# Counts copied to SBUF, places one and two pairs later, one transpose per query tile

## The chip, the core and the metric

The kernel runs on one core of a Trainium2 chip. The metric is the device time of one execution in microseconds (us). TensorE multiplies matrices (PE in the rows; PEld is its weight load), VectorE is DVE, ScalarE is ACT, GpSimd is POOL and SyncE (SP) issues most transfers.

## The reference

Causal attention for 8 batches, 12 heads, 448 positions and a head width of 64; its result, 3584 rows of 768, goes through a mixture of 8 experts. Each row picks the expert with the largest logit; its weight is that expert's softmax probability. An expert keeps the 80 rows with the largest weights among those that picked it; the other rows are zero in the output.

```
scores = where(causal, q @ k^T / 8, -1e9);  x = softmax(scores) @ v   # 12 heads side by side: [3584, 768]
expert = argmax(x @ w_gate);  gate_w = softmax(x @ w_gate)[row, expert]
for e in range(8):
    rows = the (at most) 80 rows of expert e with the largest gate_w
    out[rows] = gate_w[rows] * (relu(x[rows] @ w1[e]) @ w2[e])        # 768 -> 1024 -> 768
```

## The kernel before, in words

The work has two parts: attention for 48 head pairs (6 pairs for each of 8 batches), and then the experts, each with at most 80 rows. While attention runs, a table of the best 80 rows of every expert is kept: after each batch its rows are compared with each other and with the table, ranked, and the table is made anew.

**Order of the work.** The order is written out by hand. Every pair has eight slots (main loop, lines 1187 to 1253). Within a slot the loop puts, in this order, transposes of probabilities (`tp`, four groups in slots 0, 1, 1, 4), the product of values (`xp`, slot 5, of the pair two before), VectorE's masking with the row's smallest (`ns`, slots 0 to 4), copies of transposed probabilities (`PT`, ScalarE in slot 1 and VectorE in slot 5), ScalarE's exponentials (`prob`), ScalarE's copy of the finished values (`xu`, slot 6), and then whatever a plan has for that slot; the score products of the next pair end slot 7. Each engine carries out its instructions in that order and waits for what it needs.

**The plan of a batch.** Its steps are placed by the table `STEPS` (line 30; the seventh batch has its own table `EARLY`, the eighth a text list `TAIL`). A number is the slot counted from the end of the batch's last pair, so 42 is the third slot of the sixth pair after it; steps of two batches stand beside each other. The steps that matter:

- `columns`, `parts` (lines 831 and 843): GpSimd writes, for each of four query tiles, three copies of the one-hots of the experts (`oh3`) and five groups of 8 columns with the row's number and its weight in three bf16 parts (`mv`). They are two buffers.
- `r0t`, `r1t`, `r0c`, `r1c` (`expert_rows`, line 856): TensorE turns the one-hots and the weight columns, four transposes each into a bank of PSUM; VectorE copies 24 rows of each to `ex`.
- `rl`, `lt`, `cp`, `ro` (`table_chunk`, line 886): the table's rows against the batch's rows; `cp` counts, for each table row, the batch's rows that go ahead of it. `ro` hands `cp`, in PSUM, on.
- `places`, `places2` (`place`, line 919): VectorE makes one-hots `rm` of the table rows' new places, 80x320 in each half. They exist from the second batch on. They are used by `tn` in slot 74.
- `c3w` to `c0l` (`compare`): the batch's rows with each other (`rn`, `less`). `gt`, `own`, `rank`, `rr`: later rows counted, ranks, and the one-hot of ranks; `gt` and what `own` and `rank` make of it lie in one bank.

**Banks of PSUM.** The pool `ps_g` has four banks with one tag (line 211): `tp`, `rt` (transposed rows of the result, `row_group`, line 715), `xp`, `gp`, `selt`, `rn`, `rl`, `cp`, `gt`, `tn` take them in turn. A new tile waits until all that read the tile four before it are done.

```
STEPS = {... 'r0t': 41, 'r0c': 42, 'r1t': 42, 'r1c': 43, 'rl': 44, 'lt': 46, ... 'cp': 53, 'ro': 53, 'places': 54, ... 'places2': 54, ...}
```

Of the kernel before, what the change touches and what calls it, by code (L numbers as in the profile page):

```python
# [17 lines left out]
P = 128  # L18
# [8 lines left out]
NORMS = [0, 2, 4]  # L27
ROWS0 = [(2, 2), (3, 4), (9, 9), (19, 20)]
ROWS1 = [(27, 28), (35, 36), (36, 38), (40, 41)]
STEPS = {'gp': 20, 'gs': 22, 'lp': 24, 'lg': 25, 'logit': 26, 'shifted': 27, 'chosen': 32, 'sums': 33, 'one_hot': 33, 'columns': 33, 'weight': 35, 'weighted': 36, 'parts': 37, 'r0t': 41, 'r0c': 42, 'r1t': 42, 'r1c': 43, 'rl': 44, 'lt': 46, 'c3w': 49, 'c3l': 50, 'cp': 53, 'ro': 53, 'places': 54, 'c2w': 56, 'c2l': 57, 'places2': 54, 'c1w': 58, 'c1l': 59, 'c0w': 60, 'c0l': 61, 'earlier': 61, 'gt': 65, 'own': 67, 'rank': 67, 'rr': 68, 'tn': 73, 'tab': 74, 'rp': 76, 'row': 78}  # L30
EARLY = {'gp': 18, 'gs': 20, 'lp': 24, 'lg': 25, 'logit': 26, 'shifted': 26, 'chosen': 28, 'sums': 29, 'one_hot': 29, 'columns': 29, 'weight': 30, 'weighted': 30, 'parts': 30, 'r0t': 33, 'r0c': 34, 'r1t': 35, 'r1c': 36, 'rl': 36, 'lt': 38, 'c3w': 40, 'c3l': 41, 'c2w': 41, 'c2l': 42, 'c1w': 42, 'c1l': 43, 'cp': 43, 'ro': 43, 'c0w': 44, 'c0l': 45, 'earlier': 45, 'places': 46, 'places2': 46, 'gt': 46, 'own': 47, 'rank': 47, 'rr': 47, 'tn': 49, 'tab': 49, 'rp': 52, 'row': 53}
THIRD = [0, 0, 2, 2, 4, 6, 8]
THIRD_EARLY = [0, 2, 4, 6, 6, 8, 9]
# [139 lines left out]
def attention_then_moe(  # L173
# [12 lines left out]
    nc = tc.nc  # L186
    B, _, NP, S = qT.shape
    N, D = out.shape
    E = wg.shape[2]
# [3 lines left out]
    NT = (S + P - 1) // P  # L193
# [50 lines left out]
    SL = max(2, min(P, CAP))  # L244
    NSL = (CAP + SL - 1) // SL
    NV = 5

    COUNT = F16 if CAP + S <= 2048 else F32
    ZR = 4
# [4 lines left out]
    OFF, at = {}, 0  # L254
# [49 lines left out]
    for e, which in LAYERS:  # L304
# [4 lines left out]
        k = (K1, K2)[which - 1]  # L309
# [42 lines left out]
        return [lambda j=j, x=x: load_chunk(*got[0], j, x, 2) for j in range(k) for x in range(2)]  # L352


    mv = one_hots = mv_flat = oh_flat = expert_cols = tables = table_rows = None
    identb = before = dec = number = number_after = pnum = tbase = wgd = slots_e = slots_t = None

    tiny = const.tile([P, 1], F32, name="tiny")
# [1 line left out]
    lg = keep.tile([P, NT, (H + 1) * E], F32, name="lg")  # L360
# [35 lines left out]
    def late_constants():  # L396


        def padded(shape, name):
            t = spool.tile(shape, BF16, name=name, tag=name, bufs=1)  # L400
            nc.gpsimd.memset(t, 0.0)
            return t
# [20 lines left out]
                                          wg_sb[j * DH:(j + 1) * DH, i:NP:2, :])  # L423

        def slots():
            nonlocal mv_flat, mv
            mv_flat = padded([P, (NT - 1) * NV * E + 2 * E + P], "mv")
            mv = mv_flat[:, 0:NT * NV * E].rearrange("k (t v e) -> k t v e", v=NV, e=E)

        def operands():  # L430
            nonlocal oh_flat, one_hots, expert_cols, tables, table_rows
            oh_flat = padded([P, (NT - 1) * 3 * E + P], "oh3")
            one_hots = oh_flat[:, 0:NT * 3 * E].rearrange("k (t v e) -> k t v e", v=3, e=E)
            expert_cols = padded([P, 2, NT * P], "ex")
            tables = [[padded([SL, 2 * E + P], f"tab{s}_{i}") for i in range(2)] for s in range(NSL)]
            table_rows = [[padded([P, SL], f"row{s}_{i}") for i in range(2)] for s in range(NSL)]
# [384 lines left out]
    table = []  # L821
    rows_of = {}

    def select_groups(bt):

        b = bt.b
        last = b == B - 1
        sm = lambda name, shape, dt=F32: spool.tile(shape, dt, name=name, tag=name, bufs=1)
# [24 lines left out]

            nc.gpsimd.tensor_copy(sm("held", [P, 1]), bt.rest[:, 0, 0:1])

        def expert_rows(i):
            got = []

            def turn():
                selt = bank([P, NT * P], BF16, "selt")  # L860
                got.append(selt)
                for t in range(NT):
                    src = mv_flat[:, (t * NV + 2) * E:][:, 0:P] if i else oh_flat[:, t * 3 * E:][:, 0:P]
                    nc.tensor.transpose(selt[:, t * P:(t + 1) * P], src, identb)

            def copy():
                (nc.scalar.copy if last else nc.vector.tensor_copy)(bt.ex[0:3 * E, i], got[0][0:3 * E])
            return [turn, copy]


        def compare(t):
            w = (t + 1) * P
# [13 lines left out]
        def table_chunk(s):  # L886
            sn = min(SL, CAP - s * SL)
            got = {}
# [20 lines left out]

            def ranks():  # L910
                if NSL == 1:
                    bt.moves.append((table[s][0], got["cp"], sn))
                    return
                ro = sm(f"ro{s}", [SL, E])
                nc.vector.tensor_scalar(ro[0:sn], got["cp"][0:sn], pnum[0:sn], float(s * SL), op0=ALU.add, op1=ALU.add)
                bt.moves.append((table[s][0], ro, sn))
# [69 lines left out]
        def move(s):  # L986
# [49 lines left out]
            def row():  # L1036
# [3 lines left out]
                if s == NSL - 1:  # L1040
# [1 line left out]
            return [moved_table, one_hot, moved_last, taken] if last else [one_hot, moved, taken, turn, row]  # L1042

        bt.lower, bt.moves = [], []
        r0, r1 = expert_rows(0), expert_rows(1)
        cmp = [compare(t) for t in reversed(range(NT))]
        tabs = [table_chunk(s) for s in range(NSL)] if b else []
        moves = [f for s in range(NSL) for f in move(s)]
        steps = {"columns": columns, "parts": parts, "r0t": r0[0], "r0c": r0[1], "r1t": r1[0], "r1c": r1[1],
                 "places": places, "places2": more_places, "earlier": earlier, "own": own, "rank": rank}  # L1050
        steps.update({"hold": hold, "base": base, **{f"gt{t}": lambda t=t: later_part(t) for t in range(NT)}} if last else {"gt": later})
        for t in range(NT):
# [37 lines left out]
    for b in range(B):  # L1090
        bt = Batch()
# [94 lines left out]
    parts = []  # L1186
    for i, pr in enumerate(pairs):
        bt = pr.bt
# [76 lines left out]
    bt = batches[-1]  # L1265
# [314 lines left out]
```

## Time and profile before

| | us |
|---|---|
| median of 3 runs | 450.36 (448.03 to 450.75) |
| the profiled execution | 449.43 |
| its span, first to last instruction | 447.7 |
| TensorE busy | 428.3 (96%) |
| ScalarE busy | 391.7 (87%) |
| VectorE busy | 383.2 (86%) |
| GpSimd busy | 237.7 (53%) |

Busy times are of the one profiled execution; the rest of its 449.43 us lies around the span. A matmul's end is modelled, so the distance between starts says more of TensorE than the length of a record. Idle time is shown in brackets with what ended it.

### The profile page before, as it was taken

What the parts mean: (1) busy time and instruction counts of PE and PEld (TensorE: products, weight loads), DVE (VectorE), ACT (ScalarE), POOL (GpSimd) and SP (SyncE); (2) the same over time, 40 slices, a digit from 0 to 9 for tenths busy, and PEclk for the clock granted to TensorE, in tenths of its full rate; (3) what the DMA queues carried; (4) which work ended last, traced back from release to release, by engine and by line L of the source; (5) the groups of instructions that cost most, each with busy time, mean ns of one, the idle gap of its engine ahead of it and who ended that gap; (6) DMA issues with size and microseconds to landing.
All of it is one profiled execution on the core that took longest, in us unless ns stands there. A gap on an engine that the chain in (4) does not pass through costs nothing. (4 is left out here: it accounts for less than half of the span.)

```text
span 447.7 us, 15806 instructions
## 1 busy us (share of the span) xinstructions
PE 428.3 (96%) x5830; PEld 332.6 (74%) x5830; DVE 383.2 (86%) x1315; ACT 391.7 (87%) x1069; POOL 237.7 (53%) x360
## 2 busy tenths in 40 slices
PE   7899999999999999999999999999899999999993
PEld 3566777777677777767767776766559999899993
DVE  6777788979879897987999789798879999989992
ACT  5899999989889988988999898888877999899971
POOL 7967818547664843866585284622452126525521
PEclk9899999999999999999999999999989999999997
DMA  6475648758675762866666375379889999999701
GB/s 227 147 272 195 228 157 284 236 169 289 195 239 180 241 228 92 264 210 207 226 224 216 113 266 192 103 253 403 326 294 340 405 409 400 398 414 413 297 26 45
DMA packets 47823, 109.95 MB, mean 246 GB/s; under 512 B 5971, under 2 KB 24403, under 8 KB 47105
## 3 DMA queue, kind: packets, MB, share of 16 engines
q1 hardware_dynamic: 46544, 105.20, 67.0%
q0 software_dynamic: 1056, 3.51, 2.4%
q8 instruction: 46, 0.75, 0.7%
q14 instruction: 33, 0.26, 0.2%
q10 hardware_dynamic: 144, 0.23, 0.2%
HBM read 85.35 MB, written 23.99 MB: 244 GB/s over the span
## 5 line engine op out<-in xcount | busy, mean ns | idle before, releaser
L562 ACT ACTIVATE prob<-ns,nb 128x192 f32<-128x192 f32 (+3 forms) x336 | 175.4, 531 | 17.3 <-DVE nb L558 15.8
L558 DVE CUSTOM_DVE_ANT_0 ns<-sp,mask 128x192 f32<-128x192 f32 (+3 forms) x336 | 134.3, 442 | 23.2 <-PE sp L539 20.8
L596 PE MATMUL tp<-ident,prob 128*128 128x128 f32 x768 | 106.0, 279 | 0.1
L487 POOL TENSOR_TENSOR qk<-qk,qk 128x448 f16<-128x448 f32 x94 | 96.7, 1044 | 5.8 <-DVE qk L515 2.6
L1157 DVE SCALAR_TENSOR_TENSOR wl<-wraw,wh 128x768 f16<-128x768 f32 (+1 forms) x99 | 98.3, 1062 | 1.7 <-POOL wl L1506 1.6
L619 PE MATMUL xp<-PT,vt 128*64 128x448 f32 (+3 forms) x768 | 93.6, 386 | 0.2
L1151 ACT ACTIVATE wh<-wraw 128x768 f16<-128x768 f32 (+1 forms) x99 | 86.6, 936 | 7.4 <-PE hp L1445 5.2
L596 PEld LDWEIGHTS tp<-ident,prob 128*128 128x128 f32 x768 | 85.8, 143 | 2.4 <-ACT PT L601 0.5
L619 PEld LDWEIGHTS xp<-PT,vt 128*64 128x64 f32 x768 | 50.9, 136 | 44.6 <-issue 24.5
L601 ACT COPY PT<-tp 128x512 f32<-128x512 f32 x144 | 76.5, 589 | 7.6 <-PE tp L596 7.1
L539 PE MATMUL sp<-qk 64*128 64x448 f16 (+2 forms) x864 | 68.4, 298 | 2.9 <-POOL qk L487 2.1
L1446 PEld LDWEIGHTS <-wl 128*128 128x128 f16 x678 | 67.7, 100 | 2.3 <-issue 2.2
L1444 PEld LDWEIGHTS <-wh 128*128 128x128 f16 x678 | 68.2, 101 | 0.2 <-issue 0.2
L1445 PEld LDWEIGHTS <-wh 128*128 128x128 f16 x678 | 67.6, 100 | 0.7 <-issue 0.5
L562 ACT ACTIVATION_READ_ACCUMULATOR prob<-ns,nb 128x1 f32 x336 | 66.0, 196 | 0.0
L1490 POOL DMA_INDIRECT out<-yo,idx x8 | 32.7, 4086 | 51.2 <-ACT yo L1487 39.9
L539 PEld LDWEIGHTS <-qk 64*128 64x128 f16 x864 | 36.5, 94 | 17.7 <-issue 2.8
L601 DVE COPY PT<-tp 64x256 f32<-64x256 f32 x144 | 43.5, 327 | 3.2 <-PE tp L596 1.0
L1446 PE MATMUL hp<-xh,wl 128*128 128x80 f16 x336 | 37.8, 202 | 1.2 <-issue 1.2
L1445 PE MATMUL hp<-xl,wh 128*128 128x80 f16 x336 | 37.7, 202 | 0.5 <-issue 0.3
L1444 PE MATMUL hp<-xh,wh 128*128 128x80 f16 x336 | 37.9, 202 | 0.0
L1444 PE MATMUL op<-hh,wh 128*128 128x80 f16 x318 | 36.3, 202 | 0.3 <-issue 0.2
(187 smaller groups left out, 659.3 us busy)
## 6 DMA issues: line engine op xcount, KB each, us to landing
wraw<-w SPq DMA_DIRECT2D x49, 384.0 KB, 9.0
wraw<-w SPq DMA_DIRECT2D x29, 512.0 KB, 9.0
out<-mask SPq DMA_DIRECT2D x56, 192.0 KB, 2.2
qk<-k_t SPq DMA_DIRECT2D x23, 448.0 KB, 3.5
qk<-q_t SPq DMA_DIRECT2D x23, 448.0 KB, 5.0
vt<-v_t SPq DMA_DIRECT2D x24, 384.0 KB, 5.8
xs<-xr SPq DMA_DIRECT2D x42, 192.0 KB, 2.8
wraw<-w SPq DMA_DIRECT2D x24, 256.0 KB, 3.8
```

Of the source, the lines that this page charges most:

```text
L487: sub = lambda e, o, a, b: e.tensor_tensor(out=o, in0=a, in1=b, op=ALU.subtract)
L539: nc.tensor.matmul(pr.sp[t, j], a[rows, p, queries(t)], c[rows, p, FROM[t]:FROM[t] + WIDTH[t]], start=(x == 0), stop=(x == 2))
L558: nc.vector.tensor_tensor_reduce(out=ns, in0=pr.sp[x], in1=m, scale=-1.0 / 8.0, scalar=HUGE, op0=ALU.add, op1=ALU.min, accum_out=nb)
L562: nc.scalar.activation(pr.P[:, OFF[x]:OFF[x] + w], got[0], AF.Exp, bias=got[1], scale=-1.0, accum_out=pr.sums[:, h:h + 1])
L596: nc.tensor.transpose(tp[:, i * P:(i + 1) * P], f, ident)
L601: way(part_of(pr.PT, rows, to, *todims), part_of(got[0], rows, at, *dims))
L619: nc.tensor.matmul(xp[rows, c * P:S], st["vt"][:, c, p * P + j * DH:p * P + (j + 1) * DH], pr.PT[:, j, n0:n0 + w], start=(c == 0), stop=(c ...
L1151: nc.scalar.activation(hi_of[y][:, 0:src.shape[1]], src, AF.Copy, scale=SW)
L1157: nc.vector.scalar_tensor_tensor(out=lo_of[y][:, 0:n], in0=src, scalar=SW, in1=hi_of[y][:, 0:n], op0=ALU.mult, op1=ALU.subtract)
L1444: nc.tensor.matmul(o, wh[:, ws], h[:, c, :], start=begin, stop=False, skip_group_check=True)
L1445: nc.tensor.matmul(o, wh[:, ws], l[:, c, :], start=False, stop=False, skip_group_check=True)
L1446: nc.tensor.matmul(o, wl[:, ws], h[:, c, :], start=False, stop=end, skip_group_check=True)
```

## The change

The table `STEPS` gets other slots for nine steps; `r1t` is gone from it. One-hots and columns share one buffer, 96 columns to a query tile: number columns and weight parts from column 16 on (weight parts at 32), one-hots at 64. For the first six batches one 128-wide transpose per tile turns both; the copies take rows 64 and up, and 32 and up, of the one bank. For the last two batches there are still two sets of four transposes, the one for the one-hots 32 columns wide. In all batches but the last, `ro` is a ScalarE copy of the counts (80x8) to SBUF, and the places read that. In `STEPS` alone the places are moved: their first half from slot 54 to 62, their second half from 54 to 66.

```diff
-STEPS = {... 'r0t': 41, 'r0c': 42, 'r1t': 42, 'r1c': 43, 'rl': 44, 'lt': 46, ... 'cp': 53, 'ro': 53, 'places': 54, ... 'places2': 54, ...}
+STEPS = {... 'r0t': 42, 'r0c': 43, 'r1c': 43, 'rl': 45, 'lt': 47, ... 'cp': 53, 'ro': 54, 'places': 62, ... 'places2': 66, ...}
...
+    CM, CO, CW = 32, 64, 96
...
         def slots():
-            nonlocal mv_flat, mv
-            mv_flat = padded([P, (NT - 1) * NV * E + 2 * E + P], "mv")
-            mv = mv_flat[:, 0:NT * NV * E].rearrange("k (t v e) -> k t v e", v=NV, e=E)
+            nonlocal columns_of, one_hots, mv
+            columns_of = padded([P, (NT - 1) * CW + CO + P], "columns")
+            blocks = columns_of[:, 0:NT * CW].rearrange("k (t c) -> k t c", c=CW)
+            mv = blocks[:, :, CM - 2 * E:CM - 2 * E + NV * E].rearrange("k t (v e) -> k t v e", e=E)
+            one_hots = blocks[:, :, CO:CO + 3 * E].rearrange("k t (v e) -> k t v e", e=E)
...
-        def expert_rows(i):
+        def expert_rows(*which):
             got = []
+            at = [CO, CM]
+            alone = len(which) == 1
 
             def turn():
                 selt = bank([P, NT * P], BF16, "selt")
                 got.append(selt)
+                w = 32 if which == (0,) else P
                 for t in range(NT):
-                    src = mv_flat[:, (t * NV + 2) * E:][:, 0:P] if i else oh_flat[:, t * 3 * E:][:, 0:P]
-                    nc.tensor.transpose(selt[:, t * P:(t + 1) * P], src, identb)
+                    c = t * CW + (at[which[0]] if alone else 0)
+                    nc.tensor.transpose(selt[0:w, t * P:(t + 1) * P], columns_of[:, c:c + w], identb)
 
-            def copy():
-                (nc.scalar.copy if last else nc.vector.tensor_copy)(bt.ex[0:3 * E, i], got[0][0:3 * E])
-            return [turn, copy]
+            def copy(i):
+                r = 0 if alone else at[i]
+                (nc.scalar.copy if last else nc.vector.tensor_copy)(bt.ex[0:3 * E, i], got[0][r:r + 3 * E])
+            return [turn] + [lambda i=i: copy(i) for i in which]
...
             def ranks():
                 if NSL == 1:
-                    bt.moves.append((table[s][0], got["cp"], sn))
+                    ro = got["cp"]
+                    if not last:
+                        ro = sm("ro", [SL, E])
+                        nc.scalar.copy(ro[0:sn], got["cp"][0:sn])
+                    bt.moves.append((table[s][0], ro, sn))
                     return
...
-        r0, r1 = expert_rows(0), expert_rows(1)
+        rows = expert_rows(0) + expert_rows(1) if b >= B - 2 else expert_rows(0, 1)
```

## Rows read from the trace of the kernel before

**Rows 1.** Windows: length, busy us (instructions) of PE, PEld, DVE, ACT, POOL; clock, DMA share, GB/s.

```profile
180.00:220.00 40.00, 39.66 (x448) 28.80 (x448) 35.02 (x155) 36.27 (x116) 24.55 (x43) 1.00 0.66 215
350.00:400.00 50.00, 48.83 (x1047) 48.10 (x1044) 48.19 (x57) 46.31 (x72) 18.78 (x6) 1.00 1.03 403
```

**Rows 2.** Timeline of one pair with places: start, length, engine, line, operation, [idle before, ended by].

```profile
119.03 0.99 DVE L927 SCALAR_TENSOR_TENSOR rm<-cp,pnum,slots_e 80x320 bf16<-80x320 f32 x2
119.28 0.26 PE L546 MATMUL sp<-qk,corner 128*128 128x64 f16 x3
119.94 0.34 DVE L558 CUSTOM_DVE_ANT_0 ns<-sp,mask 128x192 f32<-128x192 f32 x1
120.02 1.04 PE L596 MATMUL tp<-ident,prob 128*128 128x128 f32 x8
120.32 0.46 ACT L562 ACTIVATE prob<-ns,nb 128x192 f32<-128x192 f32 x1 [1.08 <-DVE nb L558]
120.78 1.54 ACT L601 COPY PT<-tp 128x512 f32<-128x512 f32 x3
121.39 0.31 PEld L730 LDWEIGHTS rt<-ident,xu 128*128 128x128 f32 x3 [0.58 <-ACT PT L601]
...
121.98 0.56 DVE L749 TENSOR_TENSOR xr<-rt,sums 128x384 f32<-128x384 f32 x1 [0.47 <-PE rt L730]
...
122.59 0.20 PEld L619 LDWEIGHTS xp<-PT,vt 128*64 128x64 f32 x4 [0.23 <-DVE xr L749]
122.59 1.95 PE L619 MATMUL xp<-PT,vt 128*64 128x448 f32 x16
...
125.73 0.34 DVE L558 CUSTOM_DVE_ANT_0 ns<-sp,mask 128x192 f32<-128x192 f32 x1
...
125.81 0.26 PE L546 MATMUL sp<-qk,corner 128*128 128x64 f16 x3
```

**Rows 3.** Timeline of an earlier pair, TensorE around the turned one-hots and columns.

```profile
107.63 1.04 PE L596 MATMUL tp<-ident,prob 128*128 128x128 f32 x8
...
108.50 0.39 PE L864 MATMUL selt<-identb,oh 128*128 128x128 bf16 x4
...
108.95 0.62 PE L596 MATMUL tp<-ident,prob 128*128 128x128 f32 x4
```

**Rows 4.** Waits: who waited for whom, us in total, times, longest.

```profile
PE rt L730 <- ACT PT L601: 2.3, 7, 0.3
```

**Rows 5.** Instructions on the counts and on the table: ns shortest/median/longest, first and last start.

```profile
L927 DVE SCALAR_TENSOR_TENSOR rm<-cp,pnum,slots_e x14: 530/532/546, 119.0 to 323.5; 80x320 bf16<-80x320 f32 x14
...
L1030 ACT CAST tab<-tn x1: 188/188/188, 317.5 to 317.5; 80x40 bf16<-80x40 f32 x1
```

**Rows 6.** The same view of line 1157, an instruction with two SBUF inputs.

```profile
L1157 DVE SCALAR_TENSOR_TENSOR wl<-wraw,wh x99: 944/951/1226, 312.5 to 436.9; 128x768 f16<-128x768 f32 x57, 128x1024 f16<-128x1024 f32 x42
```

**Rows 7.** Timeline of the pair after that of rows 2.

```profile
126.08 1.80 POOL L515 CAST qk<-qk 128x896 f16<-128x896 f32 x2
...
127.10 0.61 DVE L558 CUSTOM_DVE_ANT_0 ns<-sp,mask 128x448 f32<-128x448 f32 x1
...
129.06 0.48 DVE L992 TENSOR_TENSOR rr<-gt,slots_t 128x320 bf16<-128x320 f32 x1
...
129.84 1.95 PE L619 MATMUL xp<-PT,vt 128*64 128x448 f32 x16
...
132.69 0.36 DVE L558 CUSTOM_DVE_ANT_0 ns<-sp,mask 128x192 f32<-128x192 f32 x1 [1.74 <-PE sp L539]
```

**Rows 8.** GpSimd beside VectorE: timeline at the start, and line 487 over the span.

```profile
4.70 1.16 DVE L487 TENSOR_TENSOR qk<-qk,qk 128x448 f16<-128x448 f32 x2
5.48 0.87 POOL L492 COPY corner<-qk 64x128 f16<-64x128 f16 x2 [1.32 <-DVE qk L487]
...
9.03 0.63 POOL L492 COPY corner<-qk 64x128 f16<-64x128 f16 x2
...
16.33 0.62 DVE L515 CAST qk<-qk 128x896 f16<-128x896 f32 x1
16.48 1.37 POOL L487 TENSOR_TENSOR qk<-qk,qk 128x448 f16<-128x448 f32 x1
...
L487 POOL TENSOR_TENSOR qk<-qk,qk x94: 1032/1040/1366, 7.1 to 286.0; 128x448 f16<-128x448 f32 x94
```

More of the change, by code (lines that the diff above doesn't have):

```diff
@@ L29 @@
 ROWS1 = [(27, 28), (35, 36), (36, 38), (40, 41)]
-STEPS = {'gp': 20, 'gs': 22, 'lp': 24, 'lg': 25, 'logit': 26, 'shifted': 27, 'chosen': 32, 'sums': 33, 'one_hot': 33, 'columns': 33, 'weight': 35, 'weighted': 36, 'parts': 37, 'r0t': 41, 'r0c': 42, 'r1t': 42, 'r1c': 43, 'rl': 44, 'lt': 46, 'c3w': 49, 'c3l': 50, 'cp': 53, 'ro': 53, 'places': 54, 'c2w': 56, 'c2l': 57, 'places2': 54, 'c1w': 58, 'c1l': 59, 'c0w': 60, 'c0l': 61, 'earlier': 61, 'gt': 65, 'own': 67, 'rank': 67, 'rr': 68, 'tn': 73, 'tab': 74, 'rp': 76, 'row': 78}
+STEPS = {'gp': 20, 'gs': 22, 'lp': 24, 'lg': 25, 'logit': 26, 'shifted': 27, 'chosen': 32, 'sums': 33, 'one_hot': 33, 'columns': 33, 'weight': 35, 'weighted': 36, 'parts': 37, 'r0t': 42, 'r0c': 43, 'r1c': 43, 'rl': 45, 'lt': 47, 'c3w': 49, 'c3l': 50, 'cp': 53, 'ro': 54, 'places': 62, 'c2w': 56, 'c2l': 57, 'places2': 66, 'c1w': 58, 'c1l': 59, 'c0w': 60, 'c0l': 61, 'earlier': 61, 'gt': 65, 'own': 67, 'rank': 67, 'rr': 68, 'tn': 73, 'tab': 74, 'rp': 76, 'row': 78}
 EARLY = {'gp': 18, 'gs': 20, 'lp': 24, 'lg': 25, 'logit': 26, 'shifted': 26, 'chosen': 28, 'sums': 29, 'one_hot': 29, 'columns': 29, 'weight': 30, 'weighted': 30, 'parts': 30, 'r0t': 33, 'r0c': 34, 'r1t': 35, 'r1c': 36, 'rl': 36, 'lt': 38, 'c3w': 40, 'c3l': 41, 'c2w': 41, 'c2l': 42, 'c1w': 42, 'c1l': 43, 'cp': 43, 'ro': 43, 'c0w': 44, 'c0l': 45, 'earlier': 45, 'places': 46, 'places2': 46, 'gt': 46, 'own': 47, 'rank': 47, 'rr': 47, 'tn': 49, 'tab': 49, 'rp': 52, 'row': 53}
@@ L246, in attention_then_moe @@
     NV = 5
+    CM, CO, CW = 32, 64, 96
+    assert 3 * E <= 32 and 2 * E <= CM
     COUNT = F16 if CAP + S <= 2048 else F32
@@ L352, in piece_parts @@
         return [lambda j=j, x=x: load_chunk(*got[0], j, x, 2) for j in range(k) for x in range(2)]
-    mv = one_hots = mv_flat = oh_flat = expert_cols = tables = table_rows = None
+    mv = one_hots = columns_of = expert_cols = tables = table_rows = None
     identb = before = dec = number = number_after = pnum = tbase = wgd = slots_e = slots_t = None
@@ L425, in slots @@
         def slots():
-            nonlocal mv_flat, mv
-            mv_flat = padded([P, (NT - 1) * NV * E + 2 * E + P], "mv")
-            mv = mv_flat[:, 0:NT * NV * E].rearrange("k (t v e) -> k t v e", v=NV, e=E)
+            nonlocal columns_of, one_hots, mv
[3 more added lines that the diff above has]
+            one_hots = blocks[:, :, CO:CO + 3 * E].rearrange("k t (v e) -> k t v e", e=E)
         def operands():
-            nonlocal oh_flat, one_hots, expert_cols, tables, table_rows
-            oh_flat = padded([P, (NT - 1) * 3 * E + P], "oh3")
-            one_hots = oh_flat[:, 0:NT * 3 * E].rearrange("k (t v e) -> k t v e", v=3, e=E)
+            nonlocal expert_cols, tables, table_rows
             expert_cols = padded([P, 2, NT * P], "ex")
@@ L1048, in select_groups @@
         moves = [f for s in range(NSL) for f in move(s)]
-        steps = {"columns": columns, "parts": parts, "r0t": r0[0], "r0c": r0[1], "r1t": r1[0], "r1c": r1[1],
+        steps = {"columns": columns, "parts": parts, **dict(zip(("r0t", "r0c", "r1t", "r1c") if b >= B - 2 else ("r0t", "r0c", "r1c"), rows)),
                  "places": places, "places2": more_places, "earlier": earlier, "own": own, "rank": rank}
```

## Prediction

> **What bounds the kernel now.** I read the engines' busy time by stretch first, to learn which engine sets the pace; then the order of time inside single head pairs; then the waits. In the attention part TensorE is busy 39.66 of 40 us at a granted clock of 1.00, and in the expert part 48.83 of 50 us beside a DMA share of 1.03 [rows 1]. So in the attention part TensorE's own instructions, and the few places where it stands still, set the length; the expert part starts when attention ends and is limited by its own products and its weight stream, so a shift of its start passes on whole. VectorE, ScalarE and GpSimd matter only where TensorE waits for them. The pattern repeats every six pairs; I work in two of them.
>
> In the pair that starts at 119.28 the two halves of the places stand on VectorE from 119.03, and the next pair's first masking starts behind them at 119.94, 0.66 after the pair's start. ScalarE idles 1.08 for it, copies the first transposes at 120.78, and TensorE's row transposes (rt) start at 121.39 having waited for that copy, because they take over its bank [rows 2]. How long is the stall? The eight transposes before rt take from 120.02 to 121.39, 1.37 us; eight like them take 107.63 to 108.50, 0.87, where nothing waits [rows 2, 3]. So 0.50 us. It occurs in five batches (places exist from the second batch on; the last two follow other tables). The wait list has seven such waits in all, and the five are among them [rows 4].
>
> **The change part by part.** *One transpose per tile.* Eight transposes of one-hots and weight columns run from 108.50 to 108.95, 0.45 us for eight [rows 3]. Four go, in six batches: 6 x 0.225 = 1.35 us, all on TensorE's path. The two copies to SBUF stay two and now follow each other one slot later; the counting product that reads them moves behind the values product, which has 1.95 us [rows 2], so nobody waits for them. In the last two batches the number of transposes stays; their narrower form I cost at nothing, under the same 56 ns each. The merged tile joins two buffers that were cleared apart, once, on GpSimd: nothing. No transfer is issued at another place, so SyncE's queue keeps its order, and GpSimd's does too: its rank step waits for the last comparison as before.
>
> *Counts copied to SBUF.* One ScalarE copy of 80x8 in six batches. The nearest row is ScalarE's 80x40 copy from PSUM, 188 ns [rows 5]. It stands behind the counting product, long done by then, and ahead of the pair's first exponential, in front of which ScalarE idled 1.08 [rows 2]; with the masking earlier that cover shrinks to about 0.2, which just holds it. Uncovered it would cost at most 0.19 where that pair's bank is late already; I take nothing. Its gain, a bank given back earlier, is worth nothing: no row shows TensorE waiting for that bank.
>
> *Places moved away.* The five stalls of 0.50 go: the masking starts at about 119.03, ScalarE's copy of the first transposes is then limited by the transposes themselves, and done before 120.9, where rt comes. That is 2.50 us off.
>
> *Places moved to.* The first half now stands between the last comparison of that pair and the first masking of the next, the second half in the third slot of that next pair. What is late there? Price of a half: two take 119.03 to 119.94, 0.455 each, with a PSUM input [rows 2]; an instruction of this kind with two SBUF inputs takes 944 ns for 768 elements [rows 6], which scaled to 320 is 0.39. Between 0.39 and 0.455 I take 0.40, since records of neighbours overlap (0.53 recorded, 0.455 apart) and the scaled figure is a recorded one.
>
> Now the two engines. With the stall gone rt starts at 120.89, and VectorE's scaling of rt, which waits for it, at 121.48 instead of 121.98. From there to the next pair's first masking VectorE has 3.75 us of work without a gap (121.98 to 125.73) [rows 2], plus the half: masking at 121.48 + 3.75 + 0.40 = 125.63. TensorE starts that pair at 125.81 - 0.50 = 125.31. So VectorE, which was 0.08 ahead there, is 0.32 behind. From that masking to the end of the one-hot of ranks (rr) VectorE takes 129.06 + 0.48 - 125.73 = 3.81 [rows 2, 7]; the second half lies inside it: 125.63 + 3.81 + 0.40 = 129.84, or 4.53 after the pair's start. TensorE wants the values product (xp) 129.84 - 125.81 = 4.03 after it [rows 2, 7]. Four banks rotate; counting back from this xp (gp, tp, rt, gt) it takes over the bank of the later counts gt, and rr reads its ranks from that bank. That a values product waits for VectorE in this way is seen one pair earlier, where its weight load waited for the scaling, 0.05 after its end [rows 2]. So xp comes at 4.58, a stall of 0.55 us. The same lateness also reaches that pair's rt by way of ScalarE's copies, with a smaller delay that lies ahead of xp and is contained in it.
>
> *The port.* The counts in SBUF give the places two SBUF inputs. Where VectorE took the difference of two SBUF tiles until 5.86, GpSimd's two copies from 5.48 needed 0.87 against 0.63 for the same two elsewhere; where VectorE's cast ran 16.33 to 16.95, GpSimd's difference from 16.48 needed 1.37 against a median of 1.04 [rows 8]. In both, the later one is lengthened by what the earlier had left, less 0.14: 0.38 left gives 0.24, 0.47 left gives 0.33. The second half arrives 127.10 - 125.73 = 1.37 after the masking, 1.69 into the pair, while GpSimd's two casts run from 0.27 to 2.07 into it (126.08, 1.80 long) [rows 7]: 0.38 left, so 0.24 more. Stall 0.79, in five batches 3.95 us. Its ends: nothing, if VectorE catches up unseen, and 1.83, if GpSimd's next 1.04 us difference gets in first. [...]
>
> **The sum.** -1.35 - 2.50 + 3.95 = +0.10. The profiled execution took 449.43 (span 447.7), 0.93 under the median of the runs shown, 450.36, and the four times average 449.64. From 449.43 the sum gives 449.5, and I predict that: the change moves a stall to the next pair, where it is longer, and the transposes saved pay for the difference.
>
> **Rivals.** *No port conflict* (0.20): the stall in the later pair is 0.55; 449.43 - 1.35 - 2.50 + 2.75 = 448.3. For it: places lie beside GpSimd's long differences now without growing (530 to 546 ns) [rows 5], but with one SBUF input; against it: rows 8.
> *Both stalls gone* (0.15): VectorE idles 1.74 at the end of the later pair [rows 7], so if xp doesn't hang on rr, nothing is late: 449.43 - 3.85 = 445.6. Against it: the rotation of four banks, which rows 2 bear out.
> *Slower* (0.12): the second half waits behind GpSimd's cast and then behind the difference that follows it; the stall before xp is 0.55 + 0.24 + 1.04 = 1.83, and 449.43 - 3.85 + 9.15 = 454.7. It decides from a stall of 0.77 per batch on, where the two savings (0.50, and 1.35/5 = 0.27) are eaten; halfway, with the casts merely shifted by a waiting first half (0.40), it is 1.19 and 451.5. For it: GpSimd works without a gap there.
> *The change doesn't act* (0.03): the early stall stays for another reason, ScalarE's new copy for one, and the later one comes on top: about 452.
>
> **How the numbers follow.** The forecast has 0.50. The range 446.2 to 451.7 holds it, the rival without the port and the half-way slower case, with the 1.4 us by which single runs lie apart; the rest is under 0.2. About 4.5 us (1%) is what a measurement here can tell from no change. Both stalls gone misses that by 0.6 and passes it only with a lucky run: faster 0.07. Slower by over 1% needs the full slower rival: 0.06. Within 1%: 0.87.
>
> **What would show it.** After: four transposes per batch instead of eight at that place, no wait of rt for ScalarE's copy in the pair after the counts, that pair 6.0 instead of 6.5 us; the following pair, 7.25 before, at 8.0, with a wait of xp's weight load on rr; places longer than 0.53 where they meet GpSimd. Wrong, if that pair stays at 7.25, or if an engine outside these two pairs delays TensorE.

## The result, and the profile after

The changed kernel takes 453.12 us, median of 20 runs (449.63 to 454.77), beside 449.94 for the kernel before in the same comparison (20 runs, 448.03 to 456.31). The ratio is 1.0067 [1.0054, 1.008] (it leaves out one slow execution, 456.31, 1.8% above the fastest of its kernel): 0.7% slower, inside the 1% that the prediction called no change, but 3.6 us above its forecast of 449.5 and outside its range of 446.2 to 451.7. The profiled execution took 452.79 (span 451.1), 3.36 above that of before.

The head of the page after, with each engine's busy time, share and instructions, and the queue of the instruction fetches (packets, MB, share):

```profile
PE 428.5 (95%) x5806; PEld 332.3 (74%) x5806; DVE 386.0 (86%) x1315; ACT 392.1 (87%) x1075; POOL 242.7 (54%) x359
...
q8 instruction: 45, 0.74, 0.6%
```

The windows of [rows 1], in the kernel after:

```profile
180.00:220.00 40.00, 39.47 (x445) 28.89 (x443) 35.22 (x153) 36.04 (x115) 24.53 (x44) 1.00 0.62 207
350.00:400.00 50.00, 48.76 (x1050) 48.06 (x1047) 48.00 (x56) 46.74 (x74) 22.79 (x6) 1.00 1.02 387
```

TensorE still sets the pace in both parts, and both windows look like before. The loss is in short places that such windows average away, so I measured from pair start to pair start (the product of sp with the corner), before and after:

| stretch | before | after | change | forecast |
|---|---|---|---|---|
| pair with the turned tiles (five batches) | 6.12 | 5.99 | -0.13 | -0.225 |
| pair after it | 6.43 | 6.55 | +0.12 | 0 |
| pair where the places were | 6.52 | 5.96 | -0.56 | -0.50 |
| pair where the second half of the places is now (in the fifth batch 7.34 before, so +0.83) | 7.25 | 8.17 | +0.92 | +0.79 |
| first batch's pair with the turned tiles, once | 5.97 | 5.74 | -0.23 | -0.225 |
| start of the last pair | 301.29 | 302.78 | +1.49 | +0.10 |
| from there to the first expert product (hp) | 33.15 | 34.90 | +1.75 | 0 |
| from there to the end | 113.29 | 113.40 | +0.11 | 0 |

The last three rows add up to the 3.36 within rounding. So 1.5 us come from the attention part, where the two forecast stalls went and came and the sizes were off, and 1.75 from a place that the prediction had costed at nothing.

**The stall that went.** TensorE and ScalarE in the pair of [rows 2], one batch later, kernel after (start, length, instruction):

```profile
158.71 1.04 PE L598 MATMUL tp<-ident,prob 128*128 128x128 f32 x8
158.75 1.73 ACT L603 COPY PT<-tp 128x512 f32<-128x512 f32 x3 [0.18 <-PE tp L598]
...
159.59 0.49 PE L732 MATMUL rt<-ident,xu 128*128 128x128 f32 x3
```

The eight transposes before rt take 158.71 to 159.59, 0.88, against the 1.37 that the prediction read from [rows 2]. The waits of rt for ScalarE's copy, seven before (2.3 us on the products, [rows 4]), are two:

```profile
PEld rt L732 <- ACT PT L603: 0.9, 2, 0.6
...
PE rt L732 <- ACT PT L603: 0.5, 2, 0.3
```

**The transposes.** The place of [rows 3], kernel after:

```profile
108.34 0.39 PE L869 MATMUL selt<-identb,columns 128*128 128x128 bf16 x4
108.56 0.61 PE L598 MATMUL tp<-ident,prob 128*128 128x128 f32 x4
109.10 0.60 PE L621 MATMUL xp<-PT,vt 128*64 128x448 f32 x2
```

Four transposes take 0.22 instead of eight in 0.45, as forecast. But the four tp transposes behind them now take 0.54 until the next instruction, where they took 0.45 before: 0.09 of the gain is handed on.

**The stall that came.** The pair after, which answers to [rows 7], kernel after:

```profile
163.86 0.54 DVE L936 SCALAR_TENSOR_TENSOR rm<-ro,pnum,slots_e 80x320 bf16<-80x320 f32 x1
...
163.94 0.26 PE L548 MATMUL sp<-qk,corner 128*128 128x64 f16 x3
...
164.08 0.38 POOL L976 TENSOR_TENSOR rank<-base,parts 128x4 f32<-128x4 f32 x1 [4.90 <-DVE less L886]
...
164.33 0.34 DVE L560 CUSTOM_DVE_ANT_0 ns<-sp,mask 128x192 f32<-128x192 f32 x1
164.41 1.80 POOL L517 CAST qk<-qk 128x896 f16<-128x896 f32 x2
...
165.70 0.85 DVE L936 SCALAR_TENSOR_TENSOR rm<-ro,pnum,slots_e 80x320 bf16<-80x320 f32 x1
...
168.31 0.48 DVE L1001 TENSOR_TENSOR rr<-gt,slots_t 128x320 bf16<-128x320 f32 x1
...
168.87 0.23 PEld L621 LDWEIGHTS xp<-PT,vt 128*64 128x64 f32 x4 [0.76 <-issue]
168.90 1.95 PE L621 MATMUL xp<-PT,vt 128*64 128x448 f32 x16 [0.52 <-issue]
```

The pair starts at 163.94. Its first masking starts 0.39 after that, behind the first half of the places; the second half, which meets GpSimd's two casts, takes 0.85 instead of 0.54; rr ends at 168.79 and xp's weights start 0.08 later, 4.93 into the pair (4.03 before). Note the label: the trace ascribes xp's wait to "issue". That it is rr that holds it is read from the times here, and shown by the first experiment.

**The expert part.** The first rows of the first expert are gathered by GpSimd (xg), turned by TensorE (xtp) and multiplied (hp). Ahead of them TensorE runs warming products (wp), on which nothing depends. The timeline there, kernel before:

```profile
328.42 1.08 POOL L1357 DMA_INDIRECT xg<-xs,idx  x1 [4.07 <-DMA out<-mask]
...
333.41 0.58 PE L1373 MATMUL xtp<-ident,xg 80*128 80x80 f32 x6
...
334.44 0.34 PE L1441 MATMUL hp<-xw,wraw 128*128 128x80 f32 x2
```

and kernel after:

```profile
329.91 1.07 POOL L1366 DMA_INDIRECT xg<-xs,idx  x1 [4.04 <-DMA out<-mask]
...
335.93 0.76 PE L1382 MATMUL xtp<-ident,xg 80*128 80x80 f32 x6 [2.50 <-DMA xg<-xs,idx]
...
337.68 0.56 PE L1450 MATMUL hp<-xw,wraw 128*128 128x80 f32 x2
```

The gather is issued 1.49 later, which is the attention part's shift. But the first transpose of the rows starts 6.02 after the issue instead of 5.00, and TensorE idles 2.50 for it. The rows themselves land 6.0 after the issue instead of 3.8; before, TensorE was still at its warming products then. Why is seen in the transfers. Here are the queues in the 3.5 us from the gather's issue (packets, MB, share of the 16 DMA engines), before:

```profile
q1 hardware_dynamic: 414, 0.70, 70.6%
q0 software_dynamic: 64, 0.03, 3.9%
```

after:

```profile
q1 hardware_dynamic: 492, 0.98, 100.2%
```

The gather travels in q0. Before, 64 of its packets moved in that time; after, none did, and the weight stream in q1 held the engines the whole time (100.2%, against 70.6% before). Before, this goes with an accident on SyncE, the queue that issues the weight transfers. Its first weight issue there, before:

```profile
328.53 1.64 SPq L334 DMA_DIRECT2D wraw<-w  x1
```

and after:

```profile
330.04 0.39 SPq L336 DMA_DIRECT2D wraw<-w  x1
```

Before, this one issue lasted 1.64 instead of about 0.4, so the second weight issue came 1.74 behind the first instead of 0.49, and the engines had room for the gather. At that moment a block of instructions was being fetched by DMA. The queues from 327.9 to 330 in the kernel before have the row

```profile
q8 instruction: 1, 0.02, 4.6%
```

and in the kernel after the same stretch has no such row: its fetch came at about 321, 9.0 us before the gather. TensorE has 24 products and their weight loads fewer after, so whatever is fetched by count comes at another place. That it is TensorE's own code that is fetched is an estimate from counts: 46 such blocks go with its 11660 products and weight loads before, 45 with 11612 after, and in the two windows of [rows 1] 3 and 8 blocks go with 896 and 2091 of them, while VectorE has 155 and 57 instructions there.

The kernel after also ran its first expert products at half speed, at a granted clock of 0.50. Windows of 3.41 us around TensorE's half-speed stretch (length, busy us of PE, PEld, DVE, ACT, POOL, granted clock, DMA share, GB/s), before:

```profile
327.00:330.41 3.41, 3.41 (x14) 1.42 (x13) 1.50 (x6) 3.41 (x5) 1.80 (x3) 0.50 0.85 290
```

after:

```profile
336.31:339.72 3.41, 3.41 (x17) 2.85 (x16) 2.86 (x4) 0.70 (x2) 0.96 (x1) 0.50 1.06 336
```

Before, the stretch at 0.50 lay on warming products that nobody waits for; after, it came when TensorE had idled 2.50 for the gather, and lay on the first transposes, on the three wp products behind them and on the first hp products. The step from the first transpose to the first hp product is therefore 1.75 instead of 1.03. So the +1.75 to that product is 1.02 of the gather and 0.72 of the clock.

### The profile page after: what moved, and what is told of

It reads as the page before. It is cut to its first block, busy times and chain, and to the rows that moved or that the text cites. A ratio compares the mean times of both kernels' runs of the same rounds, so it can differ in the third digit from the quotient of the medians.

```text
span 451.1 us, 15758 instructions
## 1 busy us (share of the span) xinstructions
PE 428.5 (95%) x5806; PEld 332.3 (74%) x5806; DVE 386.0 (86%) x1315; ACT 392.1 (87%) x1075; POOL 242.7 (54%) x359
## 4 chain that ended last, share of the span: by engine, by line
PE 87%; DVE 3%; DMA 3%; ACT 2%; issue 2%; POOL 2%; SPq 0%; POOLq 0%; ACTq 0%
PE xp L621 19%; PE tp L598 18%; PE sp L541 13%; PE rt L732 5%; PE hp L1453 3%; PE hp L1454 3%; PE hp L1455 3%; PE hp L1450 3%; PE op L1455 3%; PE op L1454 3%; PE op L1453 3%; PE gp L682 2%; PE op L1450 2%; PE sp L548 2%; DMA xg<-xs,idx 1%
## 5 line engine op out<-in xcount | busy, mean ns | idle before, releaser
L489 POOL TENSOR_TENSOR qk<-qk,qk 128x448 f16<-128x448 f32 x94 | 98.1, 1058 | 4.2 <-DVE qk L517 1.0
L1499 POOL DMA_INDIRECT out<-yo,idx x8 | 37.4, 4680 | 50.7 <-ACT yo L1496 40.2
L1455 PE MATMUL op<-hh,wl 128*128 128x80 f16 x318 | 36.3, 202 | 0.6 <-issue 0.5
```

The lines of the kernel that those rows point to most:

```text
L489: sub = lambda e, o, a, b: e.tensor_tensor(out=o, in0=a, in1=b, op=ALU.subtract)
L1455: nc.tensor.matmul(o, wl[:, ws], h[:, c, :], start=False, stop=end, skip_group_check=True)
```

## The experiments

My theory for the attention part: xp waits for rr, rr is late because both halves of the places stand ahead of it on VectorE, and the second is lengthened by GpSimd's casts beside it (0.85 instead of 0.54). The prediction calls this the port; what the two engines share there, no run shows. The rival: xp is late for another reason (ScalarE's added copy, the order of banks, the merged tile). For the expert part: the code fetch's place decides how soon the first gather moves. Rivals: it only shifts with attention, or the half-speed clock makes the difference. In the runs below, "after the gather" is the time from the gather's issue to the first transpose.

**both_late.** Both halves go behind rr; nothing else differs from the kernel after.

```diff
-STEPS = {... 'places': 62, ... 'places2': 66, ...}
+STEPS = {... 'places': 70, ... 'places2': 71, ...}
```

> Both halves of the places go to the last two slots of the pair after (slots 70 and 71), where VectorE idles 1.55 us before the next masking. Theory A (VectorE's work ahead of the one-hot of ranks holds the bank that the values product takes): the third pair of a batch falls from 8.17 to about 7.25 us and the second stays at 5.96, so the last pair starts 4.6 us earlier than in the changed kernel, at about 298.2, and the time is near 448.5. Rival B (the copies and the new bank order are what delays that pair): it stays near 8.1 and the time near 453.

Measured: 447.26 (9 runs, 445.54 to 448.25) against 450.02, ratio 0.9934 [0.9912, 0.9956], 1.2 under the time expected, with the last pair at 298.15 as expected. The pair with the stall, kernel both_late:

```profile
162.92 0.26 PE L548 MATMUL sp<-qk,corner 128*128 128x64 f16 x3
...
166.18 0.48 DVE L1001 TENSOR_TENSOR rr<-gt,slots_t 128x320 bf16<-128x320 f32 x1
...
166.96 1.95 PE L621 MATMUL xp<-PT,vt 128*64 128x448 f32 x16
```

rr ends at 166.66, xp starts 4.04 into the pair (4.03 before), and the pair is 7.25 again, while the pair before it keeps its gain (5.96). So the whole +0.92 is the places ahead of rr; the merged tile, the copy to SBUF and the single transposes have no part in it.

**first_early.** Only the first half stays ahead of the masking.

```diff
-STEPS = {... 'places2': 66, ...}
+STEPS = {... 'places2': 71, ...}
```

> Only the second half of the places moves away (to slot 71); the first half stays at slot 62, ahead of the next pair's first masking. Theory A: VectorE starts that pair 0.4 us late and the one-hot of ranks ends 0.77 us earlier than in the changed kernel; the pair takes about 7.45 us, held by ScalarE's late copies instead (0.2 to 0.3 over 7.25). Rival (the second half costs nothing): 8.17 stays.

Measured: 450.88 in one run; the pair takes 7.57, 0.32 over 7.25 and 0.12 over the expected 7.45. The first masking is 0.39 late, as in the kernel after, but rr ends 4.08 into the pair and xp starts 4.36 into it, so rr does not hold it. TensorE falls behind earlier: against both_late, rt, the transposes behind it and gp start 0.14, 0.27 and 0.33 later in the pair, and the two last wait for ScalarE's copies (0.18 and 0.17 in the kernel after, where the first half stands in the same slot). That is the way of the lateness that the prediction had named and left out of the sum as contained.

**second_early.** One half alone, in the later pair beside GpSimd's casts.

```diff
-STEPS = {... 'places': 62, ... 'places2': 66, ...}
+STEPS = {... 'places': 66, ... 'places2': 71, ...}
```

> One half of the places alone stands in the third slot of the pair (slot 66), the other at slot 71. Theory A: VectorE starts the pair in time, the half takes 0.77 us beside GpSimd's cast, the one-hot of ranks ends about 0.35 us after the values product would start; the pair takes 7.5 to 7.7 us. Rival (only the late start matters): 7.25.

Measured: 448.59 in one run; the pair takes 7.40, less than expected, since this time GpSimd's casts were lengthened and not the half. Timeline, kernel second_early:

```profile
161.82 0.20 POOL L976 TENSOR_TENSOR rank<-base,parts 128x4 f32<-128x4 f32 x1 [4.89 <-DVE less L886]
161.96 2.36 POOL L517 CAST qk<-qk 128x896 f16<-128x896 f32 x2
162.98 0.54 DVE L936 SCALAR_TENSOR_TENSOR rm<-ro,pnum,slots_e 80x320 bf16<-80x320 f32 x1
```

The half takes its plain 0.54 and GpSimd's two casts take 2.36 instead of 1.80. The second cast takes 1.48 instead of 0.93. It is recorded from 162.83, 0.15 ahead of the half but with the first cast running until 162.89, so which of the two was first is not shown. The expectation had fixed the loser; here it is GpSimd. In the kernel after, where the records do not overlap so, the later one loses: the rank behind the first half (0.38 instead of 0.20), the second half behind a cast (0.85 instead of 0.54).

**hold_pool.** A small GpSimd copy that waits for rr is put into GpSimd's queue, to keep its casts away from the second half.

```diff
+STEPS = {... 'rr': 68, 'held': 68, ...}
...
+        def wait_rr():
+            nc.gpsimd.tensor_copy(sm("held", [P, 1]), rr_of[0][:, 0, 0:1])
...
+                 **({"held": wait_rr} if 0 < b < B - 2 else {}),
```

> The changed kernel with one added GpSimd copy of a single column that waits for the one-hot of ranks, so that GpSimd's casts of the next third start behind it. If the port between VectorE and GpSimd lengthens the second half: it returns from 0.85 to 0.53 us and the third pair falls from 8.17 to about 7.85. If the half is long for another reason (its SBUF input): it stays at 0.85 and the pair at 8.17.

Measured: 452.29 in one run, the half 0.85 and the pair 8.17 as in the kernel after. Timeline, kernel hold_pool:

```profile
163.10 1.80 POOL L517 CAST qk<-qk 128x896 f16<-128x896 f32 x2
164.40 0.85 DVE L937 SCALAR_TENSOR_TENSOR rm<-ro,pnum,slots_e 80x320 bf16<-80x320 f32 x1
164.87 2.28 POOL L489 TENSOR_TENSOR qk<-qk,qk 128x448 f16<-128x448 f32 x2
...
167.56 0.19 POOL L1056 CAST held<-rr 128x1 f32<-128x1 bf16 x1 [0.41 <-DVE rr L1003]
```

It tells nothing apart: the casts and two differences stood ahead of the added copy in the queue.

**hold_pool2.** The same, and in those pairs GpSimd's work for the next input is handed over four slots later, so that it stands behind the copy.

```diff
...
+        late = 4 if slot >= 20 * SLOTS and slot // SLOTS % NP == 2 else 0
...
-            later_on(slot + x, [f])
+            later_on(slot + x + late, [f])
```

> As the run with the added GpSimd copy, but the split of the next third moved four slots later in five pairs, so that its casts really stand behind that copy and GpSimd is idle while the second half of the places runs. Port theory: that half falls from 0.85 to 0.54 us, and the pair from 8.17 to about 7.85. Rival (VectorE's half is long by itself there): 0.85 and 8.17 stay.

Measured: 449.45 in one run. Timeline, kernel hold_pool2:

```profile
164.54 0.54 DVE L937 SCALAR_TENSOR_TENSOR rm<-ro,pnum,slots_e 80x320 bf16<-80x320 f32 x1
...
167.39 0.19 POOL L1056 CAST held<-rr 128x1 f32<-128x1 bf16 x1 [4.09 <-DVE rr L1003]
...
167.51 1.80 POOL L517 CAST qk<-qk 128x896 f16<-128x896 f32 x2
```

With the casts gone from beside it the half takes 0.54 and the pair 7.86: 0.31 less, exactly what the half had grown by. The casts' share of the +0.92 is thus 0.31; the rest is VectorE's lateness by two halves. The delayed casts cost 0.41 in a later pair (8.11 instead of 7.70).

**before_again.** The kernel before, unchanged, profiled once more.

> The kernel before, profiled once more. In its first profile the issue of the first weight transfer after attention took 1.64 us instead of 0.4 and the second followed late, so the first gather was through at 4.99 us after its issue; in the changed kernel and its variants it took 5.80 to 6.25. If that is a property of this program, it is seen again (gather to first transpose 4.9 to 5.1); if it was chance, about 6.0, and then the expert part of the changed kernel is not slower for this reason.

Measured: 450.41. The first transpose comes 4.56 after the gather, under the 4.9 to 5.1 expected, the issue of the weight transfer beside the fetch lasts 1.56, and from the last pair to the first product it is 33.21. The accident is seen in both profiles of the kernel before, so it is hardly chance.

**one_transpose.** Only the merged tile and the single transposes; counts in PSUM and places where they were.

```diff
-STEPS = {... 'ro': 54, 'places': 62, ... 'places2': 66, ...}
+STEPS = {... 'ro': 53, 'places': 54, ... 'places2': 54, ...}
...
-                    ro = got["cp"]
-                    if not last:
-                        ro = sm("ro", [SL, E])
-                        nc.scalar.copy(ro[0:sn], got["cp"][0:sn])
-                    bt.moves.append((table[s][0], ro, sn))
+                    bt.moves.append((table[s][0], got["cp"], sn))
```

> Only the shared buffer, the one transpose per tile and the steps moved with it; counts stay in PSUM and the places at slot 54. Theory A: the sixth pair of a batch gains 0.13 us and the first of the next loses 0.12 (seen in the changed kernel), the stall of 0.5 in the second stays, so attention ends where it did (first batch alone gains 0.2). If the expert part of the kernel before had a lucky first gather, the time is 1 to 1.7 us above the kernel before; if not, it is the same within 0.3.

Measured: 451.42 (10 runs, 447.97 to 455.56) against 450.02, ratio 1.0039 [1.0012, 1.0066]. The median is 1.40 above that of the kernel before, as the expectation had it for a lucky gather, though the attention part of the profile is shorter (pairs of 5.99, 6.55, 6.40 and 7.25, against 6.12, 6.43, 6.52 and 7.25). The first transpose comes 6.50 after the gather: with fewer instructions on TensorE alone the gather is late. But the profiled execution is the fastest of the ten, 447.97, faster than the kernel before: its half-speed stretch lies in the warming (at 325.9), and from the last pair's start to the end it takes 145.82, against 146.44 before. A late gather alone did not make that execution slow, and where the slower nine lost their time was not profiled.

**after_warm.** The kernel after with 38 warming products instead of 25 ahead of the gathered rows.

```diff
-gt1 c0l gt0 earlier own *5 rank rr tn tab *25
+gt1 c0l gt0 earlier own *5 rank rr tn tab *38
```

> The changed kernel with 38 instead of 25 warming matmuls at the end of attention, so that TensorE is busy until the first gather lands. If the half-speed stretch (336.3 to 339.7 in the changed kernel) costs time because it falls on the experts' first products, it is moved ahead of them and the kernel gains 1 to 1.5 us (451.6 to 452.1). If that stretch is hidden by the weight transfers: 453, unchanged.

Measured: 451.87 (10 runs, 450.81 to 454.07), ratio 1.0042 [1.0024, 1.006], 1.25 less than the kernel after and within what was expected. The half-speed stretch lies in the warming again, at 327.6; the gather is as late as in the kernel after (it lands 6.1 after its issue, and the first transpose, behind the longer warming, starts after 6.80). Its first product is no earlier (35.10 after the last pair's start, against 34.90); the gain is behind it (111.53 from there to the end, against 113.40). From the last pair's start to the end it takes 146.63, 0.19 more than the kernel before (146.44): with the half-speed stretch off the experts' products the loss of the expert part is gone in this profile, without an earlier gather.

**after_padded.** The kernel after with 48 instructions more on TensorE at the very start, of which nothing depends: three of nine idle products go, 27 short ones come.

```diff
-    for _ in range(9):
+    for _ in range(6):
...
+    for _ in range(27):
+        nc.tensor.matmul(idle[:, 0:32], corners[0][:, 0, 0, :], corners[0][:, 0, 0, 0:32], start=True, stop=True)
```

> The changed kernel with TensorE's stream brought back to the number of instructions of the kernel before: of the 9 idle products at the start 6 stay and 27 of 32 columns are added. Theory B (the position of a 16 KB instruction fetch in TensorE's stream sets when the first gather of the experts runs): the fetch falls on the gather's issue again (within 0.5 us of it, as in both profiles of the kernel before; 9 us ahead of it in the changed kernel), the issue of a weight transfer takes 1.5 us instead of 0.4, the first transpose of gathered rows comes 4.5 to 5.0 us after the gather's issue instead of 6.0, and the median falls by about 1.4 us, from 453.1 to 451.7. Rival (the fetch has no part in it): 6.0 and 453 stay.

Measured: 450.11 (10 runs, 449.32 to 452.46) against 450.21, ratio 1.0009 [0.9984, 1.0033]: 3.0 less than the kernel after, more than the expected gain. The queues in the 3.5 us from the gather's issue, kernel after_padded:

```profile
q1 hardware_dynamic: 447, 0.80, 77.4%
q0 software_dynamic: 64, 0.03, 5.1%
q8 instruction: 1, 0.02, 1.9%
```

The fetch is back on the gather, the weight issue beside it lasts 1.27, the 64 packets go out, the first transpose comes after 3.57, no half-speed stretch lies near it (the clock is 1.00 from 296 to 344), and the first product starts 31.79 after the last pair, though the pair with the stall is still 8.17.

**before_padded.** The same padding in the kernel before.

> The kernel before with the same 48 instructions added to TensorE's stream. Theory B: the fetch leaves the gather's issue by several us, the first transpose of gathered rows comes 5.8 to 6.3 us after that issue instead of 4.6 to 5.0, and the median rises by about 1.4 us to 451.4. Rival: 450.0 stays.

Measured: 453.78 (7 runs, 452.27 to 456.62), ratio 1.009 [1.0061, 1.012]: 3.6 slower, again more than expected. The queues in the 3.5 us from the gather's issue, kernel before_padded:

```profile
q1 hardware_dynamic: 467, 0.97, 96.5%
```

The fetch lies 4.1 ahead of the gather, the weight issues last 0.40, no packet of the gather moves, the first transpose comes after 5.89, and half-speed stretches of 3.4 and 6.8 us stand at 324.3 and 334.6, the second on the first transposes and products. The fetch meets another issue on SyncE now, one of the writes of the mask into `out` for whose landing the gather waits. Timeline, kernel before_padded:

```profile
324.78 2.08 SPq L446 DMA_DIRECT2D out<-mask  x1
```

Its neighbours last 0.43 to 0.47, and the gather is issued 28.82 after the last pair's start instead of 27.12. Padding changed in opposite directions what two kernels take, and each time the fetch's place went with it.

**late_padded.** both_late with the padding.

> Both halves of the places in the last two slots of the following pair, and TensorE's stream padded as in the padded changed kernel. Both theories together: the attention part as with both halves late (last pair at 298.2), the first gather 1 to 1.5 us sooner: 445.8 to 446.3 us, 0.8 to 0.9% under the kernel before. Rival (fetch without part): 447.3.

Measured: 446.33 (6 runs, 445.2 to 447.46), ratio 0.991 [0.9887, 0.9933]: 0.9% faster than the kernel before, and faster than the kernel after by 6.8. The fetch is on the gather again (0.14 ahead of it), the weight issue lasts 1.19, and the first transpose comes after 4.75 instead of 5.80. The median is 0.93 under that of both_late, but the intervals of the two ratios overlap, so the gain itself is not clear of the noise.

**late_warm.** both_late with 38 warming products.

> Both halves late, and 38 instead of 25 warming matmuls. In the changed kernel the longer warming gave 1.2 us. If TensorE's idle time before the first gathered rows, and the half-speed stretch after it, cost that time here too: 446 to 446.5. If the late places already put the stretch into the warming: 447.3, no gain.

Measured: 447.28 (12 runs, 445.32 to 450.68), ratio 0.9949 [0.9926, 0.9973]: no gain over both_late (447.26). There the half-speed stretch lay in the warming already (at 322.6; here at 322.0), so there was nothing to cover.

All fourteen profiles together, by the place of the fetch and of the half-speed stretch (us; one execution each):

| | fetch on the gather: before, before_again, after_padded, late_padded | fetch elsewhere, half speed in the warming: one_transpose, after_warm, both_late, late_warm, hold_pool2 | fetch elsewhere, half speed on the first products: after, first_early, second_early, hold_pool, before_padded |
|---|---|---|---|
| idle of TensorE before the first transpose | 0 to 0.43 | 0 to 1.50 | 2.50 to 2.98 |
| gather to first transpose | 3.57 to 5.00 | 5.75 to 6.80 | 5.89 to 6.25 |
| first transpose to first product | 1.03 to 1.08 | 1.03 to 1.08 | 1.71 to 2.06 |
| last pair to first product | 31.79 to 33.21 | 34.14 to 35.10 | 34.90 to 36.77 |
| last pair to the end | 146.42 to 147.64 | 145.82 to 148.35 | 148.30 to 151.08 |

Up to the first product the fetch sorts them: 33.21 at most where it falls on the gather, 34.14 at least elsewhere, whatever the clock. At the end of the program the first two columns no longer differ (146.8 and 146.9 on average), and the third is about 3 us longer (149.7). So the late gather by itself is nearly made up by the end, and what goes with the loss is the half-speed stretch on the first products; before each of those five stretches TensorE had idled for the gather, 2.50 to 2.98. after_warm says the same: no idle time, gather late, loss gone. The fetch and the clock are thus not rivals but links of one chain, as far as one profile each can tell.

**What stays open.** The padding moved the medians by 3.0, 3.6 and, in both_late, 0.9 us. In the profiles of the first two pairs this is not the first gather alone. Between after and after_padded the last pair starts 1.29 sooner, the stretch to the first product is 3.11 shorter and the rest 1.41 longer; between before and before_padded they are 1.20 sooner, 3.62 longer and 1.03 longer, and of the 3.62 the later issue of the gather is 1.70, the way to the first transpose 0.89 and the half-speed stretch behind it 1.03. The earlier last pair comes from the first seven pairs and not from the padding, for hold_pool, which has none, starts its last pair at the same 301.49 as after_padded. What sets the time from the first product to the end (111.05 to 115.42) was not traced.

## Why the prediction was wrong

**Right:** the two large mechanisms in the attention part, the stall that goes and the stall that comes. The stall of rt went, from five batches, and it was worth 0.56 rather than 0.50 (0.49 of it the transposes before rt, the rest not traced). The new stall stands where it was placed, before xp and on rr, as both_late shows. The lengthening that the prediction calls the port counts: the half takes 0.85 beside GpSimd's casts and 0.54 without them, and the rival without it, 448.3, falls with hold_pool2. The rival of both stalls gone falls too, but both_late, which moves the places behind rr, does make both go. The slower rival wanted the half to wait for a difference as well; the half took 0.85, so it did not act, though the measured time lies between its half-way case (451.5) and its full one (454.7); that is chance, as most of the excess arose elsewhere.

**Mis-sized:** the term +3.95 came to 4 x 0.92 + 0.83 = 4.5. The half took 0.47 between its neighbours (163.86 to 164.33), not 0.40 (the scaled row was the wrong choice; the 0.455 read from PSUM was nearer), so the first masking was 0.39 late and not 0.32; and xp's product came 0.11 after rr's end, not 0.05. The 0.31 by which the half grew was forecast as 0.24 from two rows, one of them a cast with a single input, and a little of it was made up on the way: from that masking to rr's end it took 4.46, and 4.45 was forecast. The term -1.35 nearly vanished. Each batch gained 0.13 (the 0.09 handed on to the next transposes is missing) and lost 0.12 in the following pair, which had been costed at nothing: "the two copies to SBUF stay two" did not ask whether each still costs the same. They now follow each other and take longer until the next instruction. VectorE before,

```profile
109.81 0.41 DVE L867 COPY ex<-selt 24x512 bf16<-24x512 bf16 x1
110.15 0.60 DVE L558 CUSTOM_DVE_ANT_0 ns<-sp,mask 128x448 f32<-128x448 f32 x1
```

and after:

```profile
186.94 0.86 DVE L873 COPY ex<-selt 24x512 bf16<-24x512 bf16 x2
187.84 0.62 DVE L560 CUSTOM_DVE_ANT_0 ns<-sp,mask 128x448 f32<-128x448 f32 x1
```

Before, the next instruction started 0.34 after a copy of 0.41 began, overlapping its end. After, two copies and the next start take 0.90, 0.45 each, with no overlap: the next instruction starts 0.04 after the second copy's end. Why the overlap is gone was not shown, and that these 0.2 us make the whole +0.12 was not tested by itself.

With these sizes the attention part alone gives 449.43 + 1.49 = 450.9, inside the range.

**Wrong:** the step "a shift of its start passes on whole", with which the expert part stood at nothing in the sum. In the profile it took 1.75 more than its shift up to the first product: the first transpose came 1.02 later after the gather's issue, for which TensorE idled 2.50 behind the weight stream, and the half-speed stretch on the transposes and the products behind them cost 0.72 more. The prediction counted what the change does to each engine's work and to the order of transfers, found none moved, and took the expert part as a block. It did not ask what the fewer instructions themselves move: the place of a code fetch, as the padded kernels show. Of the signs that it named for being wrong, an engine outside these two pairs that delays TensorE comes nearest to what happened. No row of the profile before shows TensorE idle there for the gather, but the 1.64 on SyncE's queue, four times the usual issue, was there to be seen, and it was a lucky delay that 48 instructions more or fewer take away.

## What to carry to other kernels

An instruction moved off one critical path should go behind the last thing that the next one waits for, not only out of the first pair: here the places cost 0.92 a batch at slots 62 and 66, and nothing at 70 and 71. Before calling a stage unchanged, look for a delay in it that is lucky (one DMA issue that lasts several times its usual, here 1.64 against 0.40) and ask whether it hangs on the length of the code; a few instructions of padding that nothing depends on are a cheap test, and here shifted the median by 3.0 and 3.6 us. Follow such a loss to the end of the program and not only to the next product: in these profiles little was left there of the late gather by itself, and about 3 us where the half-speed stretch lay on the first products. Whether a small transfer that TensorE waits for is better issued ahead of the bulk stream that fills the DMA engines (100.2% here) was not tried, and would be the next thing to try.

## What was not expected of the hardware

Code fetch: a 16 KB block fetched by DMA beside a weight transfer's issue goes with an issue of 1.64, 1.56, 1.27 and 1.19 us instead of 0.40 in the four profiles where they met at the gather, and with a mask write's issue of 2.08 instead of 0.45 in before_padded. In the whole kernel before (10 to 440 us) 14 of the 42 issues on SyncE that overlap such a fetch last over 0.8 us, and 1 of the 289 others. It is no rule: the weight issue at 361.88, inside a fetch, took its usual 0.33, and blocks of 8 KB on another queue, 0.35 and 0.80 behind the gather's issue in one_transpose and before_padded, left the issues there at 0.40. A block is one packet (45 packets, 0.74 MB in the kernel after). With the place of one of them went medians 3.0 and 3.6 us apart, by way of another engine's queue.

GpSimd beside VectorE: where a half of the places, with its two SBUF inputs, ran beside GpSimd's casts, one of the two was longer, the half by 0.31 (0.85 against 0.54) or the casts by 0.56 (2.36 against 1.80). GpSimd's 128x4 rank, 0.20 in the kernel before, took 0.38 wherever it met the first half (after, first_early, hold_pool, hold_pool2), and 0.20 again in both_late and second_early. In the kernel after the later of the two is the longer one: the rank, 0.22 behind the first half, and the second half, behind a cast; in second_early the records are too close to tell who was first.
